# One block of a diffusion transformer on one core: a new order for all steps, with the value weights first and fewer idle products

## The chip, the cores and the metric

The kernel runs on one core of one Trainium2 chip, in one launch. The metric is the device time of the launch in microseconds; a kernel's time is the median of its runs. The core has five engines with instruction streams of their own: PE (TensorE, matrix products), DVE (VectorE), ACT (ScalarE), POOL (GpSimd) and SP, which issues most transfers. Each executes its instructions in the order in which they were written; engines wait for each other by semaphores. Matrix products read SBUF and write PSUM, which has eight banks of 128 x 512 float32.

## The reference

One token sequence x of 2048 x 448 goes through two gated branches (batch 1, 16 heads of 28, hidden width 1792). The modulation comes from a vector c.

```python
sa, ca, ga, sb, cb, gb = split6(silu(c) @ w_mod)          # 448 each
h = layernorm(x) * (1 + ca) + sa
x = x + ga * A(h)
h = layernorm(x) * (1 + cb) + sb
x = x + gb * B(h)

# A: q, k, v = h @ wqkv, per head:
phi = lambda t: concat([softmax(t @ w_phi), softmax(-(t @ w_phi))])
kv, z = phi(k).T @ v, phi(k).sum(tokens)
A = ((phi(q) @ kv) / (phi(q) @ z + 1e-6)) @ wo

# B: z = gelu(h @ w_in); z1, z2 = halves of 896
g = w_sp @ layernorm(z2) + b_sp                           # w_sp: 2048 x 2048, over tokens
B = (z1 * g) @ w_out
```

Inputs and weights are bfloat16.

## The kernel before

**Tiles.** Tokens are cut into 16 tiles of 128, the 448 columns into four chunks of 112. Step `name:i` works on token tile i unless said otherwise.

**Head.** The modulation's scale 1 + ca and shift sa are folded into the projection weights, so that layernorm's output can go into the products as it is. `ct` and `ce` make the column silu(c); `csA` and `ccA` (L760) make shift and scale columns from the loads `wsa` and `wca` of w_mod; `esA` and `ecA` move them to SBUF. For values, `SHv` (L774) adds the shift as an extra row to the weights `wv`, and `SCv:0..3` (L783 on ACT, L785 on POOL, L787 on DVE) scales their four chunks. For keys and queries w_phi is folded in too: `FTk` transposes the raw weights on PE (L809), `ETk` copies them out (L813, L815), `FSk` (L826) and `FCk` make the shift's column, `PFk` multiplies by the block diagonal matrix of w_phi that `bd` builds (L836), `EPk` scales into `Wk`. The same with q. `l1s` takes a tile's mean and variance (L843, L844), `l1e` and `l1r` its reciprocal deviation, `l1a` applies them (L854). The first four tiles are transposed on PE (`X`, L867, copied by `XE`), the others by transposing transfers on SP (`T1`, L859). `du` (L725) is a run of products of zeros that nobody reads, 256 columns wide; `scb`, `gr` and `ge` make the rows of the two gates.

**Keys, values, queries.** Per tile `kM` (L877), two exponentials `kE` and `kF` on ACT (L880), `kS` (sums, L891), `kR` and `kP` (normalised features, L898), `vM` (L885) with its copy `vC` (L888), and `kA` (L908), which accumulates features times values over all tiles in PSUM. `KV` and `KZ` bring the sum to SBUF as a block diagonal. `qM` (L932) makes the query products of half the heads for four tiles, `qE` and `qF` (L937) their exponentials.

**Attention output.** Per tile `nM` (numerators and denominators, L960), `nX`, `nC`, `nS` (denominators, L968 to L977), `nT` (normalising both halves, L980), `nA` (their sum, L986), a transposing transfer `T2`, then the product with wo: `wM` adds nothing, `wN` first adds x by a product with the identity matrix (L994), both L996 for the rest. `wR` brings the new x to SBUF: on ACT a copy of PSUM (L1001), on DVE an addition of PSUM and x (L1003). A tile whose `wR` stands on ACT therefore needs `wN`. `dm` (L965) is a run of idle products of 32 columns.

**Second branch.** `wQ` (sum of squares), `l2R`, `l2r`, `l2a` (layernorm, L1029), a transposing transfer `T3`, `SHw` and `SCw` (shift and scale into w_in, four and ten pieces), `zM` (z2, L1040) with gelu `zG`, then `zQ`, `zR`, `zW`, `zN` (its layernorm, L1063); `yM` (z1 transposed, L1069) with gelu `yG`. w_sp is read transposed by 32 transfers `W` (L1077). The token mixing uses Strassen-like sums: `tT` (L1093) and `sS` make differences and sums of blocks, `P:j,p,i` is one of seven products (L1115) per pair of feature chunks, `d` adds them up (L1124), `x` multiplies by z1 (L1131); `gM` (L1136) and `gG` do the seventh chunk plainly. `oM` (L1150), `oE` (L1153) and `oD` are the output product, the last addition and the store. `guard` (L1159, L1160) reduces values to a flag, which `read` loads into every engine and `hint` uses.

**What sets the order.** A string `ORDER` lists all steps; a loop calls them one after the other, and each appends its instructions to its engines' streams. Behind `/` stands the engine of a step that can run on several (V is DVE, S is ACT, G is POOL, Y is SP), behind `@` the place in PSUM: A0 to A2 of two banks each, B0 and B1 of one. A step that reuses a place waits for the readers of what was there. Loads are `ld:name/queue`, issued in place in SP's or ACT's stream.

```python
"l1a": l1a, "T1": T1, "X": X, "XE": XE,
"wM": lambda i, slot: wM(i, slot, False), "wN": lambda i, slot: wM(i, slot, True),
```

Of the kernel before, what the change touches and what calls it, by code (L numbers as in the profile page):

```python
# [485 lines left out]
FSq@B1 l1s:5 X:3@A1 kF:1 PFq:1@A2 l1s:6 kE:1 kM:2@B0 l1s:7 SCv:3/G FCq/S EPq:1/S XE:3/S vM:1@A0 vC:1 kS:1 vM:0@B1 ld:wo/S PFq:3@A2 kF:2 PFq:2@A0 vM:3@A1
kE:2 vM:2@B0 EPq:3/S PFq:0@A2 scb l1s:9 vC:0 ld:wmga/S vC:3 EPq:0/S kM:3@B1 EPq:2/S gr:1@A1 l1s:11 l1s:13 vC:2 qM:1@A0 kE:3 kF:3 qE:1 kS:0 l1e:4,8/G l1r:4,8
kR:0 gr:0@B1 ge:0 ge:1 qF:1 qM:0@A2 l1s:8 kR:1 qE:0 l1a:6/G l1a:4/G l1a:5/G l1s:10 T1:4,6 l1a:7/G T1:6,8 kM:4@B0 kM:5@B1 l1s:12 kP:0/G l1s:15 qF:0 kS:2
kR:2 kE:4 kS:3 l1s:14 qM:2@A1 kA:0@A0 kP:1/G kR:3 kF:4 kP:3/V kE:5 qF:2 kA:1@A0 l1e:8,12/G kP:2/V W:0,4 l1e:12,16/V kM:7@B0 kF:5 kF:7 kS:4 kE:7 kS:5 kA:2@A0
kR:5 kP:5/V l1r:8,12 l1a:8/G l1a:9/G l1a:11/G kA:3@A0 kM:6@A2 vM:5@B0 vM:4@B1 wos:0/G wos:3/V l1a:10/G T1:8,10 kR:4 kS:7 qE:2 l1r:12,16 vC:5 kP:4/V kF:6  # L490
kE:6 kS:6 kR:6 kP:6/V T1:10,12 vC:4 kM:9@A1 vM:6@B0 l1a:13/G kR:7 ld:wcb/Y ld:wsb/S l1a:14/G l1a:12/G T1:12,14 kM:8@A2 kE:9 kF:8 l1a:15/G kE:8 kP:7/G vC:6
kS:8 kA:4@A0 kM:10@B1 kR:8 kF:9 kP:8/G kS:9 kE:10 kA:5@A0 T1:14,16 vM:8@A2 kF:10 vM:9@A1 kR:9 kP:9/G vC:8 vC:9 kM:11@B0 vM:7@A2 vC:7 kS:10 kM:12@A1 kE:11
kF:11 kE:12 kR:10 kA:6@A0 kA:7@A0 kS:11 vM:10@A2 kM:14@B0 kP:10/V kF:12 kR:11 vC:10 ld:wout/Y kS:12 kF:14 vM:11@A1 vC:11 ld:win0/S kM:13@B1 vM:12@A2 kR:12
# [4 lines left out]
nX:5 wQ:0/S nA:3/V wR:1/S T2:2,4 wQ:1/S W:0,6 W:1,0 nC:4 nC:5 nS:2 dm:9,3 SHw:0@B0 SCw:0,0/S nT:4 qM:6@A2 qF:6 wts:6/V nT:5 nA:4/V nA:5/V nM:7@A0 nM:6@A1
wN:3@B1 nX:7 T2:4,6 SCw:1,0/G nX:6 qE:6 wN:2@B0 wR:3/S SCw:3,1/G nC:7 wR:2/S nC:6 nS:3 SCw:2,1/V nT:7 nT:6 nA:6/V qM:7@A2 W:0,3 l2R:0,2/G wQ:3/S l2r:0,2
l2a:1/G wQ:2/S qE:7 nM:9@A0 nM:8@A1 SCw:1,1/V l2a:0/G nX:8 nC:8 wN:4@B1 wM:5@B0 nX:9 nC:9 T3:0,1 qF:7 zM:0@A2 nA:7/G l2R:2,4/G SCw:3,0/V wR:4/S gt nS:4  # L500
nT:9 T2:6,8 nT:8 nM:10@A0 wM:6@B1 zG:0 nM:11@A1 T3:1,2 nX:10 nX:11 wR:5/V l2r:2,4 l2a:3/G l2a:2/G T3:2,4 wR:6/V W:1,3 wQ:4/V zM:1@A2 nC:11 nC:10 nA:9/G
SCw:2,0/S wQ:5/S wM:7@B1 zG:1 l2R:4,6/G l2r:4,6 nA:8/V T2:8,10 yM:0,0@B0 yG:0,0 W:0,7 nM:13@A2 nX:13 nS:5 zQ:0/S nT:10 wR:7/V wQ:7/S nT:11 nA:11/V zQ:1/V
zM:2@A0 zG:2 zR:0,2/V wQ:6/S zM:3@A1 nM:12@A0 wts:0/V wM:8@B0 l2a:4/G nX:12 zG:3 nC:13 l2a:5/G T3:4,6 l2R:6,8/G nA:10/V l2r:6,8 wM:9@B1 zM:4@A1 zG:4 nC:12
nS:6 nT:13 nM:15@A2 wR:8/V T2:10,12 nT:12 wQ:8/S l2a:6/G l2a:7/G wR:9/V zW:0,2 yM:0,1@B0 nM:14@A1 nX:15 T3:6,8 W:2,3 nC:15 wts:3/G zM:5@A0 nX:14 yG:0,1
wQ:9/S nC:14 nS:7 zQ:3/S yM:0,4@B1 yG:0,4 wts:1/G nA:12/V nT:14 wN:11@B0 nA:13/V wR:11/S nT:15 yM:1,3@B1 yG:1,3 wN:10@A1 zQ:2/V W:0,5 zN:1/G yM:1,1@B1
zM:6@A2 nA:14/G zN:0/G zG:5 yG:1,1 wR:10/S nA:15/V W:2,5 wQ:11/S T2:12,14 yM:0,5@B1 T2:14,16 W:2,4 zR:2,4/V yG:0,5 wM:12@B0 wQ:10/V l2R:10,12/V l2R:8,10/V
l2r:10,12 l2a:10/V zW:2,4 zQ:4/S wM:13@A0 wR:13/V yM:1,0@B1 wR:12/V wQ:12/V W:1,1 zQ:5/S zN:2/G yG:1,0 zG:6 yM:1,5@A1 l2r:8,10 wQ:13/V l2R:12,14/G yG:1,5
wts:4/V zM:7@A0 l2a:8/V zG:7 wM:14@B0 wR:14/V wM:15@B1 W:2,2 zQ:6/S l2r:12,14 W:2,7 l2a:9/G T3:8,10 zQ:7/S yM:1,4@A1 yG:1,4 wR:15/V wQ:15/S l2a:11/V yM:0,2@A2
ld:bsp/Y T3:10,12 W:1,7 l2a:12/V zR:4,6/G zR:6,8/V zW:4,6 zN:4/G yM:0,3@B1 yM:1,6@B0 l2a:13/V yG:0,2 zN:3/V yM:1,2@A0 yG:1,6 zM:9@A2 guard@A1 yG:1,2 zG:9
zN:5/V zM:8@A0 zW:6,8 zM:10@A1 zG:8 wQ:14/V l2R:14,16/G l2r:14,16 yG:0,3 yM:2,1@B0 zG:10 zN:7/G zM:11@A0 yM:2,6@A1 zN:6/V l2a:14/V T3:12,14 zQ:8/V zQ:9/S  # L510
zG:11 yG:2,6 W:1,4 zM:13@A2 zR:8,10/G zW:8,10 wts:5/V yM:2,2@A0 zM:12@A1 zQ:11/S zQ:10/V yG:2,2 zN:8/G W:2,0 yM:2,5@B1 zG:13 l2a:15/V T3:14,16 W:1,2 yM:2,4@A2
zR:10,12/G zW:10,12 yG:2,1 zG:12 W:0,2 zQ:12/S zQ:13/V yM:3,6@A0 yG:2,4 yG:3,6 zM:14@A1 yG:2,5 W:1,5 zN:9/V zM:15@A2 yM:3,3@A0 zG:14 yG:3,3 zN:11/V zN:10/V
zG:15 zQ:14/V yM:3,0@B1 zQ:15/S yM:3,1@A1 yM:3,2@A2 yG:3,2 wts:2/V yM:2,0@A0 W:2,1 yG:3,1 yM:3,5@B0 yG:3,5 yM:0,6@A2 W:1,6 sS:0,1,0,8/V sS:0,2,0,8/V yG:2,0
# [4 lines left out]
d:0,1,6 x:0,1,6/V d:1,0,2 P:0,2,2 tT:4,1/V read P:0,2,5 W:3,6 W:3,7 P:0,1,7 d:0,2,4 W:3,3 P:1,1,1 d:0,2,5 P:0,2,3 x:0,2,4/G sS:1,1,0,8/V sS:1,2,0,8/V d:0,2,7
d:0,2,6 gM:3@B0 d:0,1,7 gG:3 P:0,1,4 P:0,2,4 x:0,2,7/V x:0,1,7/G d:0,1,8 x:0,2,6/V oM:0,0,7@B0 x:0,1,8/G oE:0 oD:0/Y oM:1,0,7@B1 d:1,1,1 P:1,0,6 d:1,0,1
oE:1 d:1,0,3 d:1,1,2 oM:3,0,7@B0 gM:2@B1 gG:2 P:1,0,5 P:1,1,6 P:1,0,2 oE:3 sS:1,3,0,8/G P:1,0,7 oD:1/Y P:1,1,2 d:0,2,8 d:1,0,5 d:1,0,7 oM:2,0,7@B1 P:1,0,4  # L520
x:1,0,7/V x:0,2,8/G d:1,0,4 P:1,2,1 x:1,0,4/G oM:5,0,7@B0 d:1,1,3 sS:1,4,0,8/V P:1,1,5 d:1,1,5 oE:5 oD:5/Y P:1,1,7 oE:2 d:1,0,8 P:1,0,3 oM:4,0,7@B0 d:1,1,7
# [736 lines left out]
```

## Time and profile before

| | us |
|---|---|
| runs, device time | 252.49, 253.20 (median), 253.84 |
| profiled execution, device time | 252.36 |
| its span, first to last instruction | 250.5 |
| PE busy | 243.3 (97%) |
| DVE busy | 185.4 (74%) |
| POOL busy | 125.2 (50%) |
| ACT busy | 104.2 (42%) |

The span is 1.86 us shorter than the device time of the same execution. Rows of the profile have the engine, the line of the code, the operation, output and inputs by the program's names, and the shape; behind the bar the busy time, the mean of one in ns and the idle time before. A row of a timeline begins with start and duration in us, and ends with the idle time before it and what ended it. A row of busy times in stretches begins with the stretch and its length, and has behind the engines the clock that was granted to PE (1.00 is full), the busy share of the transfer engines and GB/s. The chain of waits follows the work that ended last backwards: every piece of it has start and duration, and the whole fills the span.

### The profile page before, as it was taken

Reading aid. Unit: us, or ns where it says so; the run is one execution under the profiler, and the core shown is the slowest. Engines: PE = TensorE matmul, PEld = TensorE weight load, DVE = VectorE, ACT = ScalarE, POOL = GpSimd, SP = SyncE. Lnnn points to the kernel's source line nnn. Section 1 sums busy time; section 2 is a strip of 40 time slices with the busy share of each in tenths; the row PEclk is TensorE's granted clock in tenths of the full one; section 3 lists DMA queues with packets and bytes.
Section 4 is the critical chain, followed back from the end, with each engine's and each line's share of the span. In section 5 each row is a group of like instructions: output and inputs, shape, how many; then the busy total and the mean of one; then the engine's idle time right before and its main releaser. Section 6 shows DMA issues by size and latency. Waiting matters only on the chain.

```text
span 250.5 us, 4157 instructions
## 1 busy us (share of the span) xinstructions
PE 243.3 (97%) x1517; PEld 127.0 (51%) x1517; DVE 185.4 (74%) x371; ACT 104.2 (42%) x220; POOL 125.2 (50%) x166
## 2 busy tenths in 40 slices
...
PEclk9889999999999999999999999999999999999999
...
GB/s 176 267 245 154 104 111 257 178 190 1 94 155 139 153 125 177 131 145 219 136 171 1 179 160 41 3 0 0 0 3 38 0 0 3 55 0 37 18 79 82
DMA packets 68655, 25.22 MB, mean 101 GB/s; under 512 B 58129, under 2 KB 68498, under 8 KB 68626
## 3 DMA queue, kind: packets, MB, share of 16 engines
...
q14 instruction: 15, 0.12, 0.2%
...
## 4 chain that ended last, share of the span: by engine, by line
PE 77%; DVE 12%; POOL 4%; DMA 3%; issue 1%; ACT 1%; DVEq 0%; POOLq 0%
PE g_ps L1115 29%; PE o_ps L1150 8%; PE z_ps L1069 7%; PE z_ps L1040 7%; PE g_ps L1136 6%; PE x_ps L996 3%; DVE f_ksum L891 3%; PE v_ps L885 3%; DVE f_st L843 3%; PE k_ps L877 2%; PE q_ps L932 2%; PE kvacc L908 2%; PE num L960 2%; PE warm_ps L725 2%; DMA f_hT<-f_xpad 2%; DMA f_ar<-f_ar 1%
## 5 line engine op out<-in xcount | busy, mean ns | idle before, releaser
L1124 DVE TENSOR_TENSOR f_zb<-g_ps,f_zb 128x512 f32<-128x512 f32 (+1 forms) x31 | 20.3, 668 | 18.5 <-PE g_ps L1115 18.1
L1115 PEld LDWEIGHTS <-f_z2n 128*128 128x128 bf16 x192 | 18.8, 98 | 22.5
L1131 POOL TENSOR_TENSOR f_z1T<-f_zb,f_z1T 128x512 bf16<-128x512 f32 (+1 forms) x11 | 12.0, 1102 | 35.6 <-DVE f_zb L1124 35.6
L1040 PE MATMUL z_ps<-f_ar,f_hT 112*128 112x448 bf16 (+1 forms) x128 | 26.7, 352 | 0.5 <-DMA f_hT<-f_xpad 0.5
L1069 PE MATMUL z_ps<-f_hT,f_ar 113*128 113x512 bf16 (+1 forms) x112 | 26.4, 378 | 0.1
L1150 PE MATMUL o_ps<-f_wout,f_z1T 128*128 128x448 bf16 x112 | 22.5, 352 | 0.0
L1115 PE MATMUL g_ps<-f_ar 128*128 128x512 bf16 x96 | 22.2, 379 | 0.0
L1131 POOL TENSOR_TENSOR f_z1T<-f_Sx,f_z1T 128x512 bf16<-128x512 f32 x6 | 7.3, 1221 | 26.4 <-DVE f_Sx L1124 26.4
L937 ACT ACTIVATE f_Eq<-q_ps 112x1024 bf16<-112x1024 f32 x16 | 16.2, 1037 | 6.5 <-PE q_ps L932 6.5
L1072 ACT ACTIVATE f_z1T<-z_ps 128x512 bf16<-128x512 f32 x28 | 15.9, 594 | 6.0 <-PE z_ps L1069 5.8
L1040 PEld LDWEIGHTS <-f_hT 112*128 112x128 bf16 (+1 forms) x128 | 11.9, 97 | 12.8 <-DMA f_hT<-f_xpad 2.0
L1044 ACT ACTIVATE f_zb<-z_ps 128x896 bf16<-128x896 f32 x16 | 14.6, 915 | 6.8 <-PE z_ps L1040 3.7
L980 DVE TENSOR_TENSOR f_ar<-num,f_w 128x896 bf16<-128x896 f32 x16 | 17.1, 1087 | 0.5
L1069 PEld LDWEIGHTS <-f_ar 113*128 113x128 bf16 (+1 forms) x112 | 10.8, 97 | 12.9 <-issue 0.4
L880 ACT ACTIVATE f_E<-k_ps 128x448 bf16<-128x448 f32 x32 | 16.0, 558 | 2.7 <-DVE f_phik L898 2.0
L891 DVE TENSOR_REDUCE f_ksum<-f_E 128x32 f32<-128x896 bf16 x16 | 16.6, 1051 | 0.1
L1115 PE MATMUL g_ps<-f_Eq,f_z2n 128*128 128x512 bf16 x72 | 16.7, 379 | 0.0
L1150 PEld LDWEIGHTS <-f_z1T 128*128 128x128 bf16 x112 | 10.9, 98 | 10.7
L1153 DVE TENSOR_TENSOR f_xpad<-o_ps,f_x 128x448 bf16<-128x448 f32 x16 | 9.8, 620 | 8.0 <-PE o_ps L1150 6.8
L877 PE MATMUL k_ps<-f_Wk,f_hT 113*128 113x448 bf16 (+1 forms) x64 | 15.4, 366 | 0.0
L1115 PEld LDWEIGHTS <-f_ar 128*128 128x128 bf16 x96 | 9.4, 98 | 11.2
L932 PE MATMUL q_ps<-f_hT,f_Wq 113*128 113x512 bf16 (+1 forms) x64 | 15.0, 379 | 0.0
...
## 6 DMA issues: line engine op xcount, KB each, us to landing
...
f_x<-in_A_x_dram SPq DMA_DIRECT2D x2, 448.0 KB, 8.8
f_wmg<-in_w_mod_dram ACTq DMA_DIRECT2D x2, 392.0 KB, 4.3
...
f_x<-in_A_x_dram ACTq DMA_DIRECT2D x1, 448.0 KB, 7.3
```

What stands on the lines that cost most here:

```text
L877: nc.tensor.matmul(t[:, 0, 0:D], lhsT=hT[0:KR[m], i, m, :], rhs=Wk[0:KR[m], m, :], start=(m == 0), stop=(m == KC - 1))
L880: nc.scalar.activation(out=Er[i % NR][:, s, :], in_=ps["k" + str(i)][:, 0, 0:D], func=ACT.Exp, scale=1.0 - 2.0 * s)
L891: nc.vector.tensor_reduce(out=ksum[:, i], in_=Er[i % NR][:].rearrange("p s (c f h) -> p (s c) h f", c=4, h=HP), axis=AX.X, op=ALU.add)
L932: nc.tensor.matmul(t[:, u, :], lhsT=Wq[0:KR[m], m, cc * CB:cc * CB + P], rhs=hT[0:KR[m], 4 * st:4 * st + 4, m, :], start=(m == 0), stop=(m ...
L937: nc.scalar.activation(out=Eq[st // 2][0:CB, 2 * c2:2 * c2 + 2, s, (st % 2) * 512:(st % 2 + 1) * 512], in_=ps["q" + str(n)][0:CB, :, :], f ...
L980: nc.vector.tensor_tensor(out=tr[i % 2][:], in0=numv(i)[:, :, :, 0:DH], in1=wr[i // 2 % 2][:, i % 2].unsqueeze(3).to_broadcast([P, 2, H, D ...
L1040: nc.tensor.matmul(t[:, hf, 0:D], lhsT=hT[0:KR[m], i, m, :], rhs=win_s[0:KR[m], m, FH + hf * D:FH + (hf + 1) * D], start=(m == 0), stop=(m ...
L1069: nc.tensor.matmul(t[:, 0, :], lhsT=win_s[0:KR[m], m, fc * P:(fc + 1) * P], rhs=hT[0:KR[m], 4 * st:4 * st + 4, m, :], start=(m == 0), stop ...
L1115: nc.tensor.matmul(g, lhsT=sta[:, m, :], rhs=mov[:, m, :], start=(m == 0 and i in (1, 6, 7)), stop=(m == 7), skip_group_check=True)
L1124: nc.vector.tensor_tensor(out=o, in0=x, in1=y, op=ALU.add)
L1131: eng.tensor_tensor(out=z, in0=T[r][:, c0:c1], in1=z, op=ALU.mult)
L1150: nc.tensor.matmul(ps["o" + str(t)][:, 0, 0:D], lhsT=later["z1T"][:, FO[n], t * P:(t + 1) * P], rhs=wout_s[:, FO[n], :], start=(n == 0), s ...
```

## The change

All 900 or so steps are written in a new order, many with another engine or place. The function `dm` goes, and the choice of the identity product now follows from the engine:

```diff
-    def dm(n, i):
-        for _ in range(n):
-            nc.tensor.matmul(ps["n" + str(i)][:, 1, 480:512], lhsT=zero[:, 0:P], rhs=zero[:, 0:32], start=True, stop=True)
-
...
-        "nM": nM, "nX": nX, "nC": nC, "nS": nS, "nT": nT, "nA": nA, "T2": T2, "wM": lambda i, slot: wM(i, slot, False), "wN": lambda i, slot: wM(i, slot, True),
+        "nM": nM, "nX": nX, "nC": nC, "nS": nS, "nT": nT, "nA": nA, "T2": T2, "wM": lambda i, slot, eng: wM(i, slot, eng is nc.scalar),
```

The first lines of the string, before and now:

```diff
-ORDER = """du:2@A1 ld:wk/S ld:x1/Y l1s:1 l1e:1,2/V l1r:1,2 tbl du:3@A2 ld:c/S du:3@A0 m1/G ld:x0/Y ld:wsa/Y m2a/V du:3@B1 du:14@A1 m4 ld:phi/Y du:3@B0 l1s:0 ct@B0
...
+ORDER = """du:1@B0 du:1@A2 ld:wk/Y m2a/V tbl du:2@A1 du:2@A2 du:2@A2 ld:c/S FTk:1@B0 ct@A2 ld:x0/Y l1s:0 ld:x1/S m4 ce:1 ld:x3/S ce:2 l1e:0,1/G l1r:0,1 du:8@A1 ce:3
+l1s:1 ce:4 ld:wsa/Y ld:wca/Y csA@B1 l1e:1,2/V l1r:1,2 du:8@A1 FTk:0@A2 ETk:1/V l1a:1/V ccA@B0 ld:wv/Y m1/G l1a:0/G ld:wq/S X:1@A1 ETk:0/S esA X:0@B1 ld:phi/Y
+ecA bd/V SHv@A0 SCv:1/G ld:wmga/S XE:0/S ld:x2/Y XE:1/S SCv:3/G FSk@A2 SCv:0/S FCk/S PFk:2@A1 PFk:1@B1 PFk:3@A0 EPk:1/S l1s:3 PFk:0@A2 l1s:2 SCv:2/G l1e:2,4/G
+EPk:3/S l1s:5 vM:0@B0 vC:0 vM:1@B1 EPk:2/S FSq@A0 l1r:2,4 ld:wmgb/S ld:x4/Y EPk:0/S FCq/S vC:1 l1a:2/G ld:wsb/S l1s:4 l1s:6 X:2@A1 l1a:3/G FTq:0@A2 FTq:1@B0
+XE:2/V kM:0@A1 scb ETq:0/S l1s:7 vM:2@A0 l1e:4,8/G l1r:4,8 ETq:1/S l1s:8 PFq:0@B1 kE:0 ld:x5/Y gr:0@B0 l1s:9 l1s:11 vC:2 l1a:5/G l1a:6/G l1s:10 X:3@A2
...
```

Of the idle products, 28 `du` stood ahead of the first real product; now 26 stand in the string, eight at the start, eight ahead of `csA`, eight behind it and two ahead of `zM:0`. Nine `dm` are gone. Seven tiles had the identity product, five have it now. The steps on DVE, before and now: nA 11 and 13, wR 9 and 11, wQ 5 and 4, l2a 7 and 9, zQ 6 and 7, zR 4 and 3, zN 9 and 10, wts 5 and 3, tT 10 and 5, sS 7 and 8, x 8 and 15. All four EPk stand on ACT (one before), three of the four SCv on POOL (one before), `bd` on DVE instead of POOL. `guard` stood between `yM` steps before the last T3 and stands now behind the last zM; `read` stood before the product P:0,2,5 and stands now between two oM near the end. P:0,0,1 and P:0,1,1 begin before `gM:1`. No step of the computation is left out.

SP's stream at the very start, where the loads are issued, before (`f_wm_117` is w_mod's part, `f_phi` w_phi):

```order
L655 DMA f_x<-in_A_x_dram 128x448
L654 DMA f_x<-in_A_x_dram 128x448
L650 DMA f_wm_117<-in_w_mod_dram 112x4x464
L647 DMA f_phi<-in_A_w_phi_dram 112x4x28
L656 DMA f_x<-in_A_x_dram 128x2x448
L650 DMA f_wm_117<-in_w_mod_dram 112x4x464
L643 DMA f_wv<-in_A_wqkv_dram 112x4x448
L643 DMA f_wq_raw<-in_A_wqkv_dram 112x4x448
L657 DMA f_x<-in_A_x_dram 128x4x448
```

and now:

```order
L643 DMA f_wk_raw<-in_A_wqkv_dram 112x4x448
L654 DMA f_x<-in_A_x_dram 128x448
L650 DMA f_wm_117<-in_w_mod_dram 112x4x464 x2
L643 DMA f_wv<-in_A_wqkv_dram 112x4x448
L647 DMA f_phi<-in_A_w_phi_dram 112x4x28
L656 DMA f_x<-in_A_x_dram 128x2x448
L658 DMA f_x<-in_A_x_dram 128x4x448
L659 DMA f_x<-in_A_x_dram 128x4x448
```

The key weights came from ACT's stream and lead now, the value weights are the fifth load instead of the seventh, and wq and four tiles of x went over to ACT.

ACT's stream in the head, behind the exponential of `ce:1`, before:

```order
L813 COPY f_wTk<-tps 112x2x448 x2
L813 COPY f_hT<-xt_ps 128x512
L783 ACTIVATE f_Wk<-pf_ps,f_ca_134 113x448
L659 DMA f_x<-in_A_x_dram 128x4x448
L783 ACTIVATE f_wv<-sh_ps,f_ca_134 113x448
L783 ACTIVATE f_wv<-f_wv,f_ca_134 112x448
L880 ACTIVATE f_E_121<-k_ps 128x448
```

and now:

```order
L657 DMA f_x<-in_A_x_dram 128x4x448
L643 DMA f_wq_raw<-in_A_wqkv_dram 112x4x448
L813 COPY f_wTk<-tps 112x2x448
L668 DMA f_wmg<-in_w_mod_dram 112x4x448
L813 COPY f_hT<-xt_ps 128x512 x2
L783 ACTIVATE f_wv<-sh_ps,f_ca_134 113x448
L813 CAST f_wTk<-fs_ps 112x4
L783 ACTIVATE f_Wk<-pf_ps,f_ca_134 112x448 x2
L888 CAST f_vaug<-v_ps 128x16x28
L783 ACTIVATE f_Wk<-pf_ps,f_ca_134 112x448
L669 DMA f_wmg<-in_w_mod_dram 112x4x448
L783 ACTIVATE f_Wk<-pf_ps,f_ca_134 113x448
```

The value weights' shift precedes the key weights' scaling, which is now all on ACT, and the first copy of a value product (L888) stands ahead of the first exponential of a key product (L880).

DVE's stream in the attention output, around the sixth to eighth tile, before:

```order
L971 TENSOR_TENSOR f_cr_99<-num,f_Sx 128x32 x2
L787 TENSOR_SCALAR f_ar<-f_ar,f_cb_82 112x896
L975 TENSOR_TENSOR f_dn_101<-f_cr_99 128x32
L976 RECIPROCAL f_dn_101<-f_dn_101 128x32
L977 TENSOR_TENSOR f_w_103<-f_Sx,f_dn_101 128x64
L980 TENSOR_TENSOR f_ar<-num,f_w_103 128x896 x2
L1003 SCALAR_TENSOR_TENSOR f_x,f_s_87<-x_ps,f_x 128x448 x2
L1010 SCALAR_TENSOR_TENSOR f_ar,f_s_88<-f_x 128x448
```

and now (the lines behind the removed function are four lower: L967 to L982 are L971 to L986 of before, L999 is L1003, L1025 is L1029):

```order
L967 TENSOR_TENSOR f_cr_100<-num,f_Sx 128x32 x2
L971 TENSOR_TENSOR f_dn_102<-f_cr_100 128x32
L972 RECIPROCAL f_dn_102<-f_dn_102 128x32
L973 TENSOR_TENSOR f_w_104<-f_Sx,f_dn_102 128x64
L976 TENSOR_TENSOR f_ar<-num,f_w_104 128x896
L787 TENSOR_SCALAR f_ar<-f_ar,f_cb_82 112x896
L999 SCALAR_TENSOR_TENSOR f_x,f_s_87<-x_ps,f_x 128x448 x2
L976 TENSOR_TENSOR f_ar<-num,f_w_104 128x896
L787 TENSOR_SCALAR f_ar<-f_ar,f_cb_82 112x896
L1025 TENSOR_SCALAR f_xpad<-f_x,f_m_89,f_v_90 128x4x112
```

Two wR (L999), a weight scaling (L787) and an l2a (L1025) stand now between the products of one pair of tiles.

More of the change, by code (lines that the diff above doesn't have):

```diff
@@ L486 @@
[L486 to L493, printed above, removed]
@@ L498 @@
[L498 to L505, printed above, removed]
@@ L506 @@
[L506 to L513, printed above, removed]
@@ L518 @@
[L518 to L521, printed above, removed]
@@ new lines @@
+nX:7 nM:6@A0 nC:7 SCw:1,0/G wQ:1/S SCw:2,1/G l2R:0,2/G nX:6 SCw:1,1/S nA:5/V nC:6 qM:7@A2 qF:7 qE:7 l2r:0,2 nS:3 nT:7 wM:3/S@B0 l2a:0/G W:0,1 wM:2/V@B1
+T2:4,6 nT:6 nA:6/V nM:8@A1 wR:3/S nM:9@A2 wR:2/V nX:8 nC:8 nX:9 wM:4/S@A0 wM:5/S@B1 T3:0,1 nC:9 nS:4 nT:8 nA:7/G l2a:1/G wQ:3/S wQ:2/S l2R:2,4/G T2:6,8
+du:2@B0 wR:4/S zM:0@A0 wR:5/S wQ:4/S nM:11@A1 nT:9 nM:10@A2 W:1,3 gt nX:10 wM:7/V@B1 l2r:2,4 l2a:3/V nA:8/V nA:9/V wM:6/V@B0 nX:11 nC:10 nC:11 nS:5 nT:10
+zG:0 l2a:2/G wQ:5/S T3:1,2 T3:2,4 zM:1@A0 l2R:4,6/G wts:2/G T2:8,10 SCw:2,0/V zM:2@A2 wR:6/V wR:7/V zG:1 zQ:1/S zG:2 W:1,1 nM:13@A0 wM:8/V@B0 l2r:4,6 nT:11
@@ new lines @@
+SCw:3,0/V nX:13 l2a:4/V wQ:6/S l2a:5/G wQ:7/V l2R:6,8/G nA:11/V zQ:0/V l2r:6,8 yM:0,4@A1 zR:0,2/G yG:0,4 yM:0,1@B1 W:0,7 wR:8/V yG:0,1 nC:13 T3:4,6 nM:12@A2
+nX:12 nC:12 nS:6 zW:0,2 zQ:2/S l2a:6/G zM:3@A1 nA:10/V nT:13 nA:13/G T2:10,12 zG:3 zQ:3/S yM:0,2@B1 wM:9/V@B0 wR:9/V W:1,6 l2a:7/V zN:0/V zM:4@A1 yG:0,2
+wts:1/G zG:4 T3:6,8 zM:5@A0 zG:5 W:0,4 zN:1/G wM:11/V@A1 nT:12 nA:12/V wQ:8/S wM:10/V@A2 yM:0,3@B0 wts:4/G wR:11/V nM:15@A0 wQ:9/S wR:10/V nX:15 yM:1,3@B1
+yG:1,3 nM:14@A1 l2R:8,10/V l2r:8,10 nX:14 wQ:11/V wQ:10/V l2R:10,12/G l2a:9/V yM:0,6@A2 zR:2,4/G l2a:8/V yG:0,6 nC:15 yM:1,0@B1 yG:0,3 zW:2,4 nC:14 zM:6@A2
```

48 lines of the change are left out of this document (32 added, 16 removed).

## The prediction

> **What bounds the kernel now.** I read the page's totals and chain first, then busy time in stretches, then the first 40 us of TensorE (PE) one instruction group at a time, and the chain of waits in the two places where PE stands.
>
> The first lines of the page: span, busy time of the engines and granted clock.
>
> ```profile
> span 250.5 us, 4157 instructions
> PE 243.3 (97%) x1517; PEld 127.0 (51%) x1517; DVE 185.4 (74%) x371; ACT 104.2 (42%) x220; POOL 125.2 (50%) x166
> PEclk9889999999999999999999999999999999999999
> ```
>
> PE is nearly full, so reordering can only win what PE does not use well. Where that is, the busy time in stretches tells (length, then busy us of each engine, granted clock, DMA share, GB/s):
>
> ```profile
> 8.00:11.20 3.20, 3.00 (x69) 2.89 (x69) 2.98 (x12) 1.36 (x3) 2.23 (x5) 1.00 1.13 262
> 11.20:14.60 3.40, 3.40 (x15) 1.69 (x15) 1.89 (x5) 1.93 (x4) 2.36 (x4) 0.50 1.11 317
> 20.00:38.00 18.00, 17.97 (x121) 9.66 (x119) 17.31 (x35) 15.83 (x29) 17.10 (x20) 1.00 0.65 137
> 62.00:98.00 36.00, 35.87 (x271) 20.37 (x270) 33.13 (x82) 29.98 (x75) 24.83 (x43) 1.00 0.77 135
> 98.00:122.00 24.00, 23.40 (x116) 10.81 (x114) 19.01 (x57) 18.77 (x41) 16.94 (x34) 1.00 0.90 161
> 190.00:246.00 56.00, 56.00 (x274) 26.56 (x272) 30.10 (x45) 0.00 (x0) 20.26 (x13) 1.00 0.09 30
> ```
>
> From 190 us on PE has no gap, and the chain of waits shows none from 138 on. In 11.2 to 14.6 it ran at half clock, which costs half of 3.4, 1.7 us. In 62 to 98 VectorE (DVE) is busy for 33.13 of 36 us, so PE's spacing there may be DVE's. Busy time hides short waits, because ends of pipelined matmuls are modelled; the chain, which gives each group its own spacing, is sharper:
>
> ```profile
> 57.48 0.78 PE cf_ps L760 x32
> 59.06 3.47 PE q_ps L932 x16
> 62.53 0.87 PE num L960 x16
> 63.40 0.76 PE sh_ps L779 x4
> 67.92 0.22 PE num L965 x9
> 84.85 3.04 PE z_ps L1040 x16
> 88.31 1.51 PE x_ps L996 x8
> 95.82 1.10 DVE f_ar L980
> 97.00 1.11 POOL f_ar L986
> 111.10 0.59 DVE f_flg L1159
> 111.89 4.34 DMA f_hT<-f_xpad
> 130.78 7.81 PE z_ps L1069 x36
> 138.59 3.55 PE g_ps L1136 x16
> ```
>
> From the first num group to gM:1 at 138.59, PE has 128 num matmuls (8 x 0.87 = 7.0), 32 of q (6.9), 32 of columns (0.8), 16 sh (3.0), 64 x_ps (12.1), 7 identity (1.3), 9 dummies (0.2), 128 z2 (24.3) and 112 z1 (24.3): 79.9 us, from 3.04/16, 7.81/36 and so on. It takes from 56.6 to 138.6, 82.0: **2.1 us are lost there**, by the chain around 95.8 (a product on DVE, then nA on GpSimd, POOL) and around 111.1 (a reduction of the guard on DVE, then the transpose that zM waits for).
>
> **The change, part by part.** The time of the profiled execution is 252.36, span 250.5 plus 1.86 around it; the median of the runs is 253.2, 0.84 above it. I sum from 252.36 and give the forecast on the median.
>
> *PE work taken out.* Nine dummies, 0.22, and two identity matmuls, 2 x 0.19 = 0.38, are on PE's path. Two dummies of 256 columns are put before zM:0; by 0.19 for 448 columns 0.11 each. Net **-0.38**; if PE waits there anyway, between -0.6 and 0. The price: without identity matmul x is added by wR, so wR goes from ScalarE (ACT) to DVE for two tiles (below).
>
> *The head.* What stands there now, in PE's timeline, SP's and ACT's queues and the transfers:
>
> ```profile
> 1.23 4.74 PE L725 MATMUL warm_ps<-f_zero 128*128 128x256 bf16 x28 [1.23 <-DVE f_zero L683]
> 11.16 1.68 PE L774 MATMUL sh_ps<-f_wv,f_Ga 112*128 112x448 bf16 x4
> 25.06 0.92 PE L943 MATMUL gr_ps<-f_wmg,f_scb 112*128 112x448 bf16 x4
> 25.82 1.90 PE L932 MATMUL q_ps<-f_hT,f_Wq 113*128 113x512 bf16 x8
> 5.00 0.31 SPq L643 DMA_DIRECT2D f_wv<-in_A_wqkv_dram  x1
> f_wv<-in_A_wqkv_dram SPq DMA_DIRECT2D x1, 392.0 KB, 6.1
> f_x<-in_A_x_dram ACTq DMA_DIRECT2D x1, 448.0 KB, 7.3
> 12.87 0.63 ACT L783 ACTIVATE f_wv<-sh_ps,f_ca 113x448 bf16<-113x448 f32 x1 [1.17 <-PE sh_ps L774]
> L888 ACT CAST f_vaug<-v_ps 128x448 bf16<-128x448 f32 x16 | 8.3, 543 | 3.4 <-PE v_ps L885 3.3
> L813 ACT COPY f_wTk<-tps 112x896 bf16<-112x896 bf16 x2 | 1.7, 908 | 0.4 <-PE tps L809 0.4
> L785 POOL TENSOR_SCALAR f_wv<-f_wv,f_ca 112x448 bf16<-112x448 bf16 x1 | 0.7, 655 | 0.5 <-PE sh_ps L774 0.5
> ```
>
> The value weights landed at 5.00 + 6.1 = 11.1, as the last of 2,069 KB (wk, two parts of w_mod, phi, x0 to x2), and SHv (L774) began at 11.16: the load sets it. In the new order phi, x2 and 25 KB more stand behind wv; 1,820 KB remain up to it. At the 262 KB/us of 8 to 11.2 the 249 KB are worth 0.95, so wv lands at about 10.2 and SHv ends near 11.0 at full clock. Then three scalings on POOL, 3 x 0.655, free vM:0 at about 13.0; PE meanwhile has FSk and the four PFk. Before, kM:0 followed SHv at 12.6, still at half clock. From 13.0 on ACT paces the new order: one value shift 0.63, four EPk (all on ACT now), two vC, both wTq copies ahead of kE:0. Chaining these with the durations of this profile (0.63, 0.54, 0.91), the work that was finished at 25.82 (four tiles of k and v, both gate rows, the first q pair) is finished at about 25.4: **-0.4**. With another half-clock window in it I get 26.6; with cold PE up to 14.6, about 28.2. So this term lies between -1.2 (all of the 1.7 back, less ACT's waits) and +2.4.
>
> *Behind the head, to nM:0.* The one wait that PE's timeline gives there, and DVE's group of row statistics:
>
> ```profile
> 38.32 0.59 PE L908 MATMUL kvacc<-f_vaug,f_phik 128*128 128x116 bf16 x8 [0.35 <-DVE f_phik L898]
> L843 DVE BATCH_NORM_STATS2 f_st<-f_x 128x6 f32<-128x448 bf16 x16 | 9.8, 612 | 2.0 <-DMA f_x<-in_A_x_dram 1.9
> ```
>
> DVE paces this stage (17.31 of 18 us). Its list from kS:0 to kP:15 becomes shorter: four of the row statistics (L843, 0.61 each without the small step behind) that stood in it are done before kS:0, but kS:0 itself starts later, since kE:0 and kF:0 come later on ACT. I take **0**, between -0.5 (that wait gone) and +1.5 (kF:0 two us later than I think).
>
> *Middle, nM:0 to the mixing.* The list of DVE grows. The prices:
>
> ```profile
> L986 DVE TENSOR_TENSOR f_ar<-f_ar 128x448 bf16<-128x448 bf16 x11 | 4.6, 425 | 0.1
> L986 POOL TENSOR_TENSOR f_ar<-f_ar 128x448 bf16<-128x448 bf16 x5 | 5.2, 1050 | 14.5 <-DVE f_ar L980 14.5
> L1003 DVE SCALAR_TENSOR_TENSOR f_x<-x_ps,f_x 128x448 bf16<-128x448 f32 x9 | 5.5, 618 | 0.7 <-PE x_ps L996 0.6
> L1029 DVE TENSOR_SCALAR f_xpad<-f_x,f_m,f_v 128x448 bf16<-128x448 bf16 x7 | 3.7, 543 | 1.7 <-POOL f_v L1026 1.5
> L1063 DVE TENSOR_SCALAR f_z2n<-f_zb,f_zm,f_zv 128x896 bf16<-128x896 bf16 x9 | 4.2, 503 | 0.6 <-POOL f_zv L1026 0.6
> ```
>
> Two more nA (0.85), two wR (1.24), two l2a (1.09) and one zN (0.50) go to DVE; two gate products, a moment group and the guard ahead of T3 go from it or to a later place. nA gains 0.6 us of latency each time it leaves POOL, and the guard's reductions, 0.59 for the first, are no longer ahead of the transpose at 111.89. Walking through the new order with these durations I find four tight places (nM:6's slot, wM:4 behind T2, zM:2 behind T3, yM:3,1 behind the last T3) that together cost about 1.3 instead of 2.1: **-0.8**. The bounds: all 2.1 gone, or 1.5 lost on top if DVE holds each of the four up.
>
> *Mixing and the end.* PE has the products P, gM and oM there, the same in number and without a gap before. Seven tT go to POOL (two before) and seven x from POOL to DVE, which was busy for 30.10 of 56 us in 190 to 246: **0**, at worst +1.2 where P waits for a tT on POOL. The step in which every engine loads the flag moves from between two products to a place between two oM near the end; I cost it at nothing, since PE has queued work on either side, and a stall of some tenths if not.
>
> Sum: -0.38 - 0.4 + 0 - 0.8 + 0 = -1.58. From 252.36 that is 250.8, and on the median, **251.6 us**.
>
> **Rivals.** *The clock.* PE ran 28 dummies in the first 6 us; now only eight run before wk lands, and eight each around the first shift column, with waits between. If the granted clock is half for one window in the head, the sum gets +1.2 (26.6 for 25.4): 252.8; cold throughout the head, +2.8: 254.4. For it speaks that a half-clock window followed at 11.2, where PE was 94% busy from 8 to 11.2, but with short transposes and one-column products. Against it: sixteen dummies now stand at that very place. The Trainium skill, "TensorE: Matmul & The Clock Gate", Part 1, says that a free-running window of some 3.4 us decides, so that the start of the windows is chance; the window of 11.2 to 14.6 agrees in its length, and that makes this rival a matter of luck from run to run.
>
> *The queues.* x3 and wq are issued by ACT at about the same time as wca and wv by SP. If two queues share the engines evenly, rather than serve in order of issue, 784 KB go along with wca and wv, up to half of wv's rate is lost and it lands at 12.1 or later, 2 us behind my 10.2; SHv shifts by that, kM and q catch up in part, +1.6 of 2: 253.2. The trace: x5 on ACT's queue took 7.3 us, landing after all that SP had issued before it, which speaks for order of issue. In the Trainium skill, "DMA: Bandwidth & Descriptors", the section "Queues, rings and completion order" states that each engine goes round-robin over its queues by packets; by that rule the time is this rival's, and the 7.3 us do not show such sharing.
>
> *DVE in the middle* (the slower side). Its slack in 62 to 98 is 36 - 33.13 = 2.87. Counting the new list up to that point, 2.1 us more land on DVE in this stretch. If the two wR that came from ACT stand ahead of nC and nT, as they do, num's slots free later, nM waits, then T2, wM, l2a and zM after it. It decides once the wait for the PSUM slot of nM ends on DVE's products and not on PE. Then the old 2.1 stays and 2.1 comes on top: 252.36 - 0.38 - 0.4 + 2.1 = 253.7, on the median **254.5**, slower.
>
> *Nothing.* If the stretches behind the head absorb the head's gain (DVE-bound up to 54 us) and the middle's losses only change place, -0.4 is left: 252.8.
>
> **How the numbers follow.** My forecast 0.38 (251.6, itself 250.2 to 252.3); the clock with one window, the queues, or nothing, together 0.25 (252.8 to 253.2); DVE in the middle, or the late kS:0 at its +1.5 and more, 0.25 (254.5); cold head 0.12 (254.4 and more). A measurement of this kernel tells about 0.5%, 1.27 us, from no change: bounds 251.93 and 254.47. Faster: nearly nine tenths of the forecast, a quarter of the second group, a little of the rest, 0.42. Slower: four fifths of DVE's, two thirds of the cold head, some of the second group, 0.32. Same: 0.26. The range of 8 in 10 reaches from 249.9 (the middle's 2.1 all back) to 255.0 (DVE's 254.5 and a little of what may come on top).
>
> **What would show it.** SHv at 10.2 to 10.5 and the first v matmul at about 13.0 (queues: 12 and 14.5). PEclk at 9 in slices 2 to 4 (the clock). The last matmul of the first q pair and gate rows by 25.4. nM:0 at 56 or just before. The distance from nM:0 to gM:1 at 80.5 rather than 82.0; over 83 is the DVE rival, with idle PE ended by DVE rows between 60 and 100. PE without a gap from there to 246. I would be wrong above all if kS:0 comes so late that DVE ends the key stage later than 54 us.

## The result, and the profile after

The changed kernel takes 257.47 us (median of 20 runs, 253.97 to 260.35), the kernel before beside it 252.85 (20 runs, 251.60 to 256.01). The ratio is 1.0124, 95% interval 1.009 to 1.0158; it leaves out runs counted as disturbed and so is smaller than that of the medians, 1.018. It is **slower**, by 1.2%, and the interval lies wholly above 1. The forecast was 251.6, with a range of 249.9 to 255.0.

The profiled execution after is one of the quickest, 254.28, against 252.36 before: what it shows is the lower part of the loss. The page after, its first lines:

```profile
span 252.4 us, 4114 instructions
PE 242.7 (96%) x1495; PEld 127.4 (50%) x1504; DVE 193.1 (77%) x375; ACT 102.4 (41%) x217; POOL 120.1 (48%) x166
PEclk9999999999999999999999999999999999999999
```

No half-clock slice stands in it any more, PE's busy time is 0.6 shorter, and still the span is 1.9 longer. I divide it by the starts of the first num group (`nM:0`), of the first product of the mixing and of the last addition (L1153, after L1149). These rows are of the kernel before; the last is from its chain of waits:

```profile
56.48 1.00 PE L960 MATMUL num<-f_ar,f_Eq 112*128 112x120 bf16 x16
138.43 3.71 PE L1136 MATMUL g_ps<-f_Eq,f_z2n 128*128 128x512 bf16 x16
246.25 0.62 DVE f_xpad L1153
```

After, the num group starts at 57.20 and the last addition at 247.77; the row of the mixing, at 139.90, stands further down:

```profile
57.20 1.00 PE L960 MATMUL num<-f_ar,f_Eq 112*128 112x120 bf16 x16
247.77 0.62 DVE f_xpad L1149
```

That gives three stages:

| profiled execution, us | before | after |
|---|---|---|
| up to nM:0 | 56.48 | 57.20 |
| nM:0 to the first product of the mixing | 81.95 | 82.70 |
| from there to the last addition | 107.82 | 107.87 |

So 0.7 is lost in the head and keys, 0.75 between nM:0 and the mixing, and nothing from there to the last addition. The remaining 0.4 of the 1.9 lies behind the start of that addition; no run asks for its cause. The head first, in PE's timeline after:

```profile
6.10 1.89 PE L725 MATMUL warm_ps<-f_zero 128*128 128x256 bf16 x8
8.26 1.87 PE L725 MATMUL warm_ps<-f_zero 128*128 128x256 bf16 x8
11.94 1.05 PE L774 MATMUL sh_ps<-f_wv,f_Ga 112*128 112x448 bf16 x4
14.49 1.69 PE L885 MATMUL v_ps<-f_wv,f_hT 113*128 113x448 bf16 x8
16.13 0.98 PE L826 MATMUL fs_ps<-f_Ga,f_wq_raw 112*112 112x1 bf16 x16
18.02 0.92 PE L877 MATMUL k_ps<-f_Wk,f_hT 113*128 113x448 bf16 x4
```

The idle products take 1.89 us for eight, which is a start every 0.21, twice what they take at full pace (in e9 below eight take 1.05 us). PE's list is late by them, and SHv starts at 11.94, though wv landed at 9.7. FSq, the first step that reads wq, starts at 16.13. The transfer of wq, before (the first two rows: issue, then size and time to landing) and after:

```profile
5.35 0.49 SPq L643 DMA_DIRECT2D f_wq_raw<-in_A_wqkv_dram  x1
f_wq_raw<-in_A_wqkv_dram SPq DMA_DIRECT2D x1, 392.0 KB, 7.2
...
6.64 0.55 ACTq L643 DMA_DIRECT2D f_wq_raw<-in_A_wqkv_dram  x1
f_wq_raw<-in_A_wqkv_dram ACTq DMA_DIRECT2D x1, 392.0 KB, 9.4
```

5.35 + 7.2 = 12.6 before, 6.64 + 9.4 = 16.0 now: in this execution wq comes in the very moment in which PE wants it. In others it comes later, as the experiments show.

The start of the mixing in the timeline after:

```profile
137.06 6.37 POOL L1059 TENSOR_SCALAR f_z2n<-f_zb,f_zm,f_zv 128x896 bf16<-128x896 bf16 x2
137.17 2.28 DVE L1096 TENSOR_TENSOR f_ar<-f_ar,f_wsp 128x4096 bf16<-128x4096 bf16 x1
138.76 1.08 ACT L1068 ACTIVATE f_z1T<-z_ps 128x512 bf16<-128x512 f32 x2 [0.27 <-PE z_ps L1065]
139.90 3.61 PE L1111 MATMUL g_ps<-f_wsp,f_z2n 128*128 128x512 bf16 x15 [1.17 <-ACT f_z1T L1068]
```

PE stands for 1.17 us until ACT has read the last gelu's input out of PSUM: the places A0 to A2 are given up as a whole, by the step `gal`, and P:0,0,1 is the first to use what takes their room. Before, gM:1 in place B0 stood between. Now it can't: it needs all tiles of z2n, and zN:12 and zN:13 are still on POOL, in 6.37 us for two beside DVE's large sums.

### The profile page after: what moved, and what is told of

Same layout as the page of the kernel before. It is cut to its first block, busy times and chain, and to the rows that moved or that the text cites. A ratio compares the mean times of both kernels' runs of the same rounds, so it can differ in the third digit from the quotient of the medians.

```text
span 252.4 us, 4114 instructions
## 1 busy us (share of the span) xinstructions
PE 242.7 (96%) x1495; PEld 127.4 (50%) x1504; DVE 193.1 (77%) x375; ACT 102.4 (41%) x217; POOL 120.1 (48%) x166
## 4 chain that ended last, share of the span: by engine, by line
PE 85%; DVE 4%; DMA 3%; POOL 3%; issue 2%; ACT 1%; DVEq 0%; POOLq 0%
PE g_ps L1111 27%; PE z_ps L1036 9%; PE o_ps L1146 8%; PE z_ps L1065 7%; PE g_ps L1132 5%; PE k_ps L877 5%; PE v_ps L885 5%; PE q_ps L932 4%; PE x_ps L992 3%; PE kvacc L908 3%; PE num L960 2%; DMA f_wk_raw<-in_A_wqkv_dram 2%; DMA f_hT<-f_xpad 1%; PE warm_ps L725 1%; POOL f_z2n L1059 1%
## 5 line engine op out<-in xcount | busy, mean ns | idle before, releaser
L1127 POOL TENSOR_TENSOR f_z1T<-f_zb,f_z1T 128x512 bf16<-128x512 f32 (+1 forms) x9 | 10.4, 1152 | 65.2 <-DVE f_zb L1120 65.2
L880 ACT ACTIVATE f_E<-k_ps 128x448 bf16<-128x448 f32 x32 | 15.8, 564 | 2.1 <-PE k_ps L877 2.1
L1149 DVE TENSOR_TENSOR f_xpad<-o_ps,f_x 128x448 bf16<-128x448 f32 x16 | 9.9, 621 | 7.8 <-PE o_ps L1146 7.7
L898 POOL TENSOR_TENSOR f_phik<-f_E,f_kr 128x896 bf16<-128x896 bf16 x7 | 12.0, 1717 | 6.9 <-DVE f_kr L895 4.6
L877 PE MATMUL k_ps<-f_Wk,f_hT 113*128 113x448 bf16 (+1 forms) x64 | 14.5, 352 | 0.0
```

Of the source, the lines that this page charges most:

```text
L877: nc.tensor.matmul(t[:, 0, 0:D], lhsT=hT[0:KR[m], i, m, :], rhs=Wk[0:KR[m], m, :], start=(m == 0), stop=(m == KC - 1))
L880: nc.scalar.activation(out=Er[i % NR][:, s, :], in_=ps["k" + str(i)][:, 0, 0:D], func=ACT.Exp, scale=1.0 - 2.0 * s)
```

## The experiments

Each is a change of the order of steps alone. The kernel before ran beside each group; its medians there were 252.46, 252.81, 252.07 and 252.61. Where runs are set side by side, I give the mean granted clock of the run too: one window of 3.4 us at half clock takes 0.007 from it.

**e1_warm**, more idle products at the start:

```diff
-du:2@A1 du:2@A2 du:2@A2 ld:c/S
+du:2@A1 du:2@A2 du:16@A2 ld:c/S
```

> The changed kernel with 14 more idle products at the start (22 instead of 8, then a wait for wk as before), nothing else. Theory clock: in the profiled run of the change PE spaces the 256-column idle products by 0.213 us up to 9.9 us and the transposes by 0.107 up to 11.9, which is half clock, since the first eight end at 2.9 and PE stands until 4.7; with PE busy up to 4.7 the clock rises before wk lands. Then the same products between 6 and 12 us go at 0.107 and 0.05, SHv starts at 10.0 to 10.4 instead of 11.94, and the median falls by 1.5 to 3 us (to 254.5 to 256), with less spread. Rival loads or ACT: wv lands at 9.7 and ACT's list paces the head from there, so SHv starts earlier but the first q pair does not, and the median moves by less than 0.5 us. Rival chance: the clock falls back to half in a later window as in the kernel before, and the spread stays 6 us.

257.55 (6 runs, 255.57 to 260.79): nothing gained. PE in the profiled run, 258.99, and its busy time in stretches (length, PE, PEld, DVE, ACT, POOL, granted clock, DMA share, GB/s):

```profile
18.41 1.66 PE L826 MATMUL fs_ps<-f_Ga,f_wq_raw 112*112 112x1 bf16 x16 [2.89 <-DMA f_wq_raw<-in_A_wqkv_dram]
...
16.00:20.00 4.00, 1.59 (x18) 1.59 (x19) 1.80 (x6) 0.39 (x1) 1.33 (x3) 0.68 0.71 172
20.00:24.00 4.00, 4.00 (x27) 2.71 (x27) 3.28 (x10) 2.77 (x5) 1.99 (x4) 0.50 0.39 105
```

SHv came at 11.42 instead of 11.94, but PE then stood 2.89 us for wq, which landed at 18.4, and behind that wait the clock went to half. So the slow start was not what set this run's time; what a warm start alone is worth, the wait hides. The wait named the next theory.

**e2_gm_first**, the start of the mixing as it was:

```diff
 zR:12,14/G
+zW:12,14
 ...
 tT:1,2/V
+zN:12/V zN:13/V
 ...
-zW:12,14 zN:12/G
 ...
-gal P:0,0,1 zN:13/G
+gM:1@B0 gal P:0,0,1
 ...
-gM:1@B1
 ...
-gM:0@B0
+gM:0@B1
```

> The changed kernel with the start of the mixing as before: gM:1 ahead of the release of the PSUM places, zN:12 and zN:13 on DVE right after the first two tT, zW:12,14 right behind zR:12,14. Theory mixing: PE's gap of 1.55 us ahead of P:0,0,1 (138.35 to 139.90) goes, since gM:1 covers the last gelu, and the span is 1.2 to 1.6 us shorter in runs of equal clock. Rival DVE: the sums sS and tT on DVE come 1 us later by the two zN, and the gap only moves behind P:0,0,1; the span changes by less than 0.4 us.

256.10 (6 runs, 255.60 to 257.29). In five of them with a mean clock of 0.983 to 0.993 the median is 256.1; the change's ten runs below 0.995 have 257.96, so 1.9 less, somewhat more than the 1.2 to 1.6 forecast. Its profiled run has the same wait for wq as e1_warm:

```profile
17.46 1.09 PE L826 MATMUL fs_ps<-f_Ga,f_wq_raw 112*112 112x1 bf16 x16 [1.73 <-DMA f_wq_raw<-in_A_wqkv_dram]
...
16.00:20.00 4.00, 2.54 (x33) 2.54 (x34) 1.40 (x4) 1.42 (x5) 1.57 (x3) 0.77 0.70 152
20.00:24.00 4.00, 4.00 (x28) 2.34 (x27) 3.22 (x11) 3.38 (x6) 3.33 (x7) 0.80 0.29 96
```

(0.23 + 0.20) x 4 us x 2 = 3.4 us at half clock. Here nM:0 starts at 60.3, 3.1 later than in the change's own profiled run.

**e3_new_head** and **e4_new_rest** cross the two orders at nM:0; steps that one has earlier and the other later are kept once.

```diff
 e3: order of the change up to nM:0, then the order of before from nM:0
 e4: order of before up to nM:0, then the order of the change from nM:0
```

> The new order up to nM:0, the old order from there (with the steps that one has earlier and the other later kept once). Theory head: nM:0 at 57.2 in a run without a half-clock window, the distance from nM:0 to the mixing 82 as before; median 255 to 257 and the spread of the changed kernel (over 5 us), since the clock of the head is chance. Theory middle and mixing: 252.5 to 253.5, spread as before.

> The old order up to nM:0, the new order from there. Theory head: the clock as before (one half-clock window at 11), spread as before, and only the gaps behind nM:0 are left, 0.7 us at 82 and 1.3 us ahead of the first product, less 0.6 of work that is gone: 252.5 to 254. Theory middle and mixing: 254.5 to 256, most of the loss.

e3 256.48 (6 runs, 253.75 to 257.99), ratio 1.0166 (1.0127 to 1.0204); e4 253.72 (12 runs), ratio 1.0046 (1.002 to 1.0071). Most of the loss is in the head; e3's profiled run has 82.4 from nM:0 to the mixing. e4 has the gap at the mixing, as in the change:

```profile
138.21 3.61 PE L1111 MATMUL g_ps<-f_wsp,f_z2n 128*128 128x512 bf16 x16 [1.17 <-ACT f_z1T L1068]
```

**e5_wq_early**, one load elsewhere:

```diff
-ld:wq/S
 ...
-ld:phi/Y
+ld:phi/Y ld:wq/Y
```

> The changed kernel with one load moved: the raw query weights wq are issued by SP right behind phi, not by ACT behind x3. In the runs so far wq landed at 12.6 in the kernel before and at 16.1 to 18.4 with the new head, and PE, whose next step is FSq, stood for it up to 1.7 us and then had half clock from 18.5 or 20.0 on. Theory query load: wq lands at 11.3 to 12, FSq follows vM:1 at once in every run, no half-clock window behind 16 us, and the median falls by 2 to 3.5 us to 254 to 255.5, with a spread under 3 us. Rival clock alone (the windows come from the transposes and one-column products, not from the wait): FSq does not wait but the half clock at 18 to 20 stays in half of the runs, median above 256. Rival loads: x2, behind wq now, lands 1.5 us later and XE:2 and kM:2 take over the wait.

254.72 (12 runs, 254.12 to 256.45), 2.75 below the change, and not one run under a mean clock of 0.995; of the change's 20 runs ten were. wq lands at 4.56 + 6.9 = 11.5, and the stretches are full; the first two rows are the transfer:

```profile
4.56 0.31 SPq L643 DMA_DIRECT2D f_wq_raw<-in_A_wqkv_dram  x1
f_wq_raw<-in_A_wqkv_dram SPq DMA_DIRECT2D x1, 392.0 KB, 6.9
...
16.00:20.00 4.00, 4.00 (x50) 3.02 (x50) 3.57 (x10) 3.88 (x9) 3.30 (x7) 1.00 0.95 245
20.00:24.00 4.00, 4.00 (x34) 2.46 (x33) 3.86 (x10) 3.87 (x9) 3.72 (x9) 1.00 0.23 49
```

In the profiled execution nM:0 stays where it was, 57.21 for 57.20, and the change's ten runs at 0.995 and more have 254.97, 0.25 above e5. So what e5 takes away is the runs in which wq is late and a half-clock window follows: the late query weights were the main cause of the loss in the median, and the half clock was their effect.

**e6_wq_late_before**, the reverse on the kernel before:

```diff
-ld:wq/Y
+ld:x3/Y ld:x4/Y ld:wq/Y
 ...
-ld:x3/Y
 ...
-ld:x4/Y
```

> The kernel before with one load moved the other way: wq behind x3 and x4 on SP's queue. Theory query load: wq lands near 16 instead of 12.6, PE stands at FTq, and the time rises by 2 to 4 us to 254.5 to 256.5. Rival clock alone or other causes: within 0.7 us of before.

258.96 (4 runs, 256.85 to 262.62), ratio 1.0208 (1.0104 to 1.0312): 6 us more, beyond my 2 to 4. The profiled run is the best of the four:

```profile
16.48 1.74 PE L808 MATMUL tps<-f_ident,f_wq_raw 112*112 112x112 bf16 x16 [2.69 <-DMA f_wq_raw<-in_A_wqkv_dram]
...
16.00:20.00 4.00, 3.52 (x26) 2.71 (x27) 1.91 (x5) 1.35 (x2) 0.00 (x0) 0.57 0.28 73
```

Two of the others had mean clocks of 0.967 and 0.971, four windows at half or more.

**e7_wq_early_gm** has the edits of e5 and e2.

> The changed kernel with wq early and the start of the mixing as in e2_gm_first. If both terms add: 1.2 to 1.6 us below e5_wq_early in runs of equal clock, 252.7 to 254 in the median. If the mixing's gap only moves: within 0.5 us of e5_wq_early.

253.35 (12 runs, all at 0.997 or more), 1.4 below e5: the terms add. From nM:0 at 57.35 to the first product it has 81.0 us. It equals the kernel before within the uncertainty, ratio 1.002 (0.9982 to 1.0059).

**e8_wq_early_warm** has the edits of e5 and e1; **e9_loads_gm_warm** those of e7 and e1, with x2 ahead of wq; **e10_loads_gm** is e9 without e1's edit.

```diff
 e9, e10:
-ld:phi/Y
+ld:phi/Y ld:x2/Y ld:wq/Y
```

> The changed kernel with wq early and 22 idle products at the start. Theory cold start: PE ran at half clock from 4.7 to 11 us with only eight idle products; with the clock up by 7.4 as in e1_warm SHv starts at 10.0 to 10.8 instead of 11.6 to 11.9, and since nothing waits for wq now, 0.5 to 1.5 us come through to the end beside e5_wq_early. Rival ACT: the list on ACT paces the head from SHv on and the first v matmul and first k matmul move by less than 0.3 us.

> The changed kernel with the loads in the order wv, phi, x2, wq on SP, the mixing's start as in e2_gm_first, and 22 idle products at the start. In e8 a warm start with wq early only moved the wait to tile 2 (PE stood 2.15 us ahead of X:2, whose x2 came behind wq). Theory loads: with x2 at 11 and wq at 12.6 neither waits, the clock stays up, SHv starts at 10.0 to 10.8 instead of 11.8, and the median is 0.7 to 1.5 us under e10, about 252. Rival: with PE early the list on ACT or the row statistics pace the head, PE stands in it as in e8 and the next window is at half clock: median above 255.

> As e9 without the added idle products, so like e7 but with x2 ahead of wq: within 0.5 us of e7_wq_early_gm (253.35), no run with a half-clock window behind 12 us.

e8 258.28 (4 runs), e9 255.99 (12 runs), e10 253.81 (12 runs, 0.996 or more). I was wrong on the warm start twice: PE, early now, stood in the statistics of tiles 2 and 3 instead, in e8 at X:2, in e9 at kM:0, whose place in PSUM X:2's copy frees, and fell to half clock.

```profile
17.67 0.40 PE L867 MATMUL xt_ps<-f_ident,f_xpad 128*128 128x128 bf16 x4 [2.15 <-POOL f_xpad L854]
20.00:24.00 4.00, 4.00 (x16) 1.87 (x14) 3.07 (x9) 1.84 (x4) 3.37 (x7) 0.50 0.21 53
...
20.09 0.92 PE L877 MATMUL k_ps<-f_Wk,f_hT 113*128 113x448 bf16 x4 [2.58 <-DVE f_hT L815]
```

(The first two rows are e8's, the third is e9's.) With x2 in time the wait is there all the same, so the load of x2 was not its only cause; how much of it is POOL's three scalings ahead of l1a:2 wasn't tried. Three of e9's runs had no such window (mean clock 0.999 and more): 252.50, 253.97 and 254.01, their median no lower than e10's. So no run shows a gain by the warm start.

**e11_zn_only** is e5 with zN:12 and zN:13 moved as in e2, but gM:1 left where the change has it.

> As e5_wq_early, with zN:12 and zN:13 moved to DVE and zW:12,14 earlier as in e7, but gM:1 left behind the products. If the gap at the start of the mixing is the wait for the last gelu's place in PSUM, it stays at 1.2 to 1.6 us and the time that of e5 (254.7); if it is the late zN on POOL, it goes and the time is that of e7 (253.35).

256.63 (4 runs), not below e5. The gap stays:

```profile
142.20 3.61 PE L1111 MATMUL g_ps<-f_wsp,f_z2n 128*128 128x512 bf16 x16 [1.17 <-ACT f_z1T L1068]
```

So the gap is the release of PSUM and not the late zN; these only keep gM:1 from covering it. That the four runs are 1.9 above e5's median I can't lay to one cause: the profiled one shows two more waits of 0.96 and 1.58 us, for l1a:2 and for a transposing transfer, which e10's shows in part.

**e12_no_dummies** is e10 without the sixteen idle products around csA.

```diff
-du:8@A1
 ...
-du:8@A1
```

> As e10 without the sixteen idle products around csA. On e7's chain these take 3.55 us at half clock ahead of SHv. Theory clock: without them PE is idle for most of 6 to 10 us, the clock stays at half beyond 12 us, and the time rises by 1 us or more beside e10. Rival: SHv starts with the landing of wv (10.0 instead of 11.8) and the time falls by 0.5 to 1.5 us.

256.49 (4 runs, 254.60 to 258.90), 2.7 above e10. SHv started earlier, at 10.84, but its four products took 1.65 us, and the slow pace lasted: eight value products from 15.29 on took 3.19 us, against 1.69 in the change.

```profile
10.84 1.65 PE L773 MATMUL sh_ps<-f_wv,f_Ga 112*128 112x448 bf16 x4 [0.17 <-DMA f_wv<-in_A_wqkv_dram]
```

The idle products, which cost some 3.3 us of PE's time at half pace in the head, pay for themselves.

**e13_old_head_gm** is e4 with the edit of e2.

> The old order up to nM:0, the new order from there, with gM:1 ahead of the release of the PSUM places and zN:12, zN:13 on DVE. From nM:0 to the first product of the mixing e7_wq_early_gm has 81.0 us, the kernel before 81.95, e4_new_rest 82.3. Theory two causes: 81.0 to 81.3 here too, the time 0.7 to 1.2 us below the kernel before in runs of equal clock and 1.2 to 1.4 below e4, 251.3 to 252.3 in the median. Rival: the rest loses something else that the old head's timing brings out, and it stays within 0.4 us of the kernel before or above it.

251.77 (12 runs, 250.89 to 255.50), ratio 0.997 (0.995 to 0.999): **faster than both kernels**, by 0.3% of the one before.

```profile
55.48 1.00 PE L960 MATMUL num<-f_ar,f_Eq 112*128 112x120 bf16 x16
137.15 3.62 PE L1132 MATMUL g_ps<-f_Eq,f_z2n 128*128 128x512 bf16 x15
```

From nM:0 to the mixing 81.7, less than 81.95 before, but not the 81.0 to 81.3 that I expected: the new order behind nM:0 does not give the whole of e7's gain behind the old head. Of its runs at a mean clock of 0.995 and more the median is 251.67, of the kernel before 252.01 (35 runs): 0.34 less, where I had expected 0.7 to 1.2. That is within the 0.4 of my rival, by which the rest loses something else behind the old head; what, wasn't looked for.

## Why the prediction was wrong

**The value weights: right, and beside the point.** wv landed at 2.70 + 7.0 = 9.7, sooner than the 10.2 of the prediction. But SHv began at 11.94 and the first value product at 14.49, where the prediction has 10.2 to 10.5 and 13.0, since PE was behind with idle products at twice the full-pace price: I reckoned with 0.11 for 256 columns, and they took 0.21.

**The step that failed is "From 13.0 on ACT paces the new order".** That chain has every step on ACT but not the load that FSq, FTq and all behind them on PE wait for. The bytes for it stood in the prediction's own terms: 1,820 KB up to wv, then phi 25, x2 224, x4 448, x3 448 and wq 392 make 3,357 that are issued up to wq; before, wq was complete at 2,461 KB and 12.6 us. 896 KB more at 262 KB/us are 3.4 us: 16.0, as measured, though partly by luck, since the two queues didn't serve in that order (below). I followed the load that the order moved forward and not the one that it moved back. By e5 this costs 2.75 in the median, because the wait brings a half-clock window with it: 1.7 for the window, and the wait itself.

**The head's -0.4 came out as +0.7 at nM:0 even where wq came just in time.** At the prediction's own mark it was already more, some +1.2: of the four tiles of k and v, both gate rows and the first q pair, the last is a key product, done near 27.0 instead of 25.82 (the group of two tiles from 26.13 on, with the next start at 27.83). This part is not wq, for e5 has it too. Nor did an earlier SHv alone mend it: e10 has SHv at 11.40, e11 at 10.87, and nM:0 at 59.11 and 59.54, with waits of 1.6 us for a transposing transfer at 43 us. Its cause stays open.

**The clock rival happened, for another reason.** Ten of the 20 runs have a mean clock under 0.995 (median 257.96, the others 254.97). I laid it to the small number of idle products; e1 and e8 put 14 back without a gain, and e5 removed it with one load. These windows follow a wait in which PE stands, in e1, e2, e6, e8 and e9. The slow pace at the start was there as well, up to some 12 us. 14 more idle products ended it earlier (in e9 before 7.46), but no run shows a gain by that.

**The queue rival fell for wv, but the order of issue isn't kept either.** wv landed at 9.7 instead of 12.1 or later: from 6.6 to 9.7 us SP's queue moved 0.82 MB and ACT's, with x3 and wq issued at 6.21 and 6.64, nothing. From 9.7 to 12.5, though, they moved 0.63 and 0.32 MB side by side, and x5, issued by SP behind wq, at 6.73, landed at 15.5, ahead of it. In the kernel before the two queues also moved 0.67 and 0.50 MB side by side, from 12.5 to 16.0, so that x5's 7.3 us were no evidence for the order of issue. The Trainium skill's "DMA: Bandwidth & Descriptors", "Queues, rings and completion order", has the engines go round-robin over queues; by such sharing ACT's x3 and wq, 840 KB at half of 262 KB/us from 6.2 us on, would have been done near 12.6 (the prediction's 784 KB for the two is too small). In the profiled run wq took until 16.0. Neither rule gives what was seen.

**DVE in the middle: fell.** Ahead of the mixing the stretch became shorter: e7, with the gap covered, has 81.0 where before had 81.95, 0.94 less against 1.18 forecast (0.38 of PE work and 0.8 of stalls). Behind the old head, in e13, it is 81.7, only 0.25 less, so how much comes through hangs on the head. A wait of 0.56 us for a transposing transfer at 83 us, one of the four tight places, is in the profile after.

**The start of the mixing: missing in the sum.** P:0,0,1 and P:0,1,1 begin before gM:1 now, and I gave the stage nothing at its start. What gM:1 did there, fill the wait for the last gelu, I had not asked. It costs 1.4 (e7 against e5). Behind it 107.87 for 107.82: the zero held.
